# Decode attention on one core: K and V loaded in 1 MB transfers of 8 KB rows, four heads to a transfer and two transfers to a slot, slots on multiples of 512 bytes

## The chip, the cores and the metric

The kernel runs on one core of a Trainium2 chip. The metric is the device time of one execution in microseconds. Each run is called fast, or slow when it is over 1.5% above the fastest run of the same kernel.

In the profiles PE is the tensor engine (matrix products; PEld is its loading of weights), DVE the vector engine, ACT the scalar engine and SP the engine that issues the large loads. A load goes from HBM, the chip's main memory, to SBUF, the memory of 128 partitions beside the engines; 16 DMA engines carry it in packets. The granted PE clock is the share of full speed that the profile records for PE; "warm" means full clock, "cold" half.

## The reference

One decode step for 8 sequences: layer norm of `x`, attention over the last 1,024 cached tokens with 32 query heads on 8 key/value heads, and a gated feed-forward branch that multiplies the attention output.

```python
# x [8,1,512]; k_cache, v_cache [8, 8, 4096, 128]; all bf16
W = 1024                                   # min(4096, max(256, Sk // 4))
q = (layernorm(x) @ wq)                    # 32 heads of 128
k, v = k_cache[:, :, Sk-W:], v_cache[:, :, Sk-W:]   # each head serves 4 query heads
o = softmax(q @ k.T * 128**-0.5) @ v
s = o @ wo
g = silu((gelu(xn @ w_gate) * (xn @ w_up)) @ w_down)
return x + s * g
```

The tokens that are read of K and V are 33.6 MB; the weights are another 13.9 MB. Everything is read once.

## The kernel before

All large loads go through one DMA queue (the SP queue) into a ring of ten slots of 16 KB per partition. Weights are read with all 128 partitions as the outer dimension. A K or V tile is one batch, all 8 heads: partition `8p+n` holds 64 consecutive tokens of head `n`.

```python
PS = P // Hkv                     # 16 groups of 8 partitions
NCH = W // PS                     # 64 tokens in a partition
ring = tc.tile_pool(name="ring", bufs=10)
pad_t = pad.tile([P, 416 // 2], BF16)       # where the ring starts

def load_rows(src, rows, r0, n, name):      # weights
    t = ring.tile([P, n, src.shape[1]], BF16, tag="slot")
    nc.sync.dma_start(out=t, in_=src.rearrange("(p r) n -> p r n", r=rows)[:, r0:r0+n, :])

def load_cache(cache, b, name):             # K and V: 2 MB, rows of 16 KB
    t = ring.tile([P, NCH, Dh], BF16, tag="slot")
    nc.sync.dma_start(
        out=t.rearrange("p c d -> p (c d)"),
        in_=cache[b, :, win0:Sk, :].rearrange("n (p c) d -> p n (c d)", p=PS),
    )
# ... constants, layer norm, queries: cut ...
# per batch: 64 transposes of K (PE), 8 copies to SBUF (DVE), 4 mask matmuls,
# 64 score matmuls, 4 Exp (ACT), 4 sum matmuls, 64 value matmuls, 1 reduce, 1 scaling
for b in range(B):
    if b > 0:
        k_t[b] = load_cache(A_k_cache, b, "k_t")
        v_t[b - 1] = load_cache(A_v_cache, b - 1, "v_t")
    transposes(b, 0)
    # ... scores, values of the batch before, interleaved: cut ...
# ... feed-forward, output projection, final sum: cut ...
```

In memory the heads of a batch lie 1 MB apart, so the source of a K tile is 16 groups of 8 rows: rows of a group 1 MB apart, groups 16 KB apart.

The softmax here doesn't subtract the row's maximum and nothing guards it: scores larger than these inputs give would overflow.

Of the kernel before, what the change touches and what calls it, by code (L numbers as in the profile page):

```python
# [7 lines left out]
ACT = mybir.ActivationFunctionType  # L8
ALU = mybir.AluOpType
AX = mybir.AxisListType  # L10
BF16 = mybir.dt.bfloat16
FP32 = mybir.dt.float32

NEG = -1.0e30
# [3 lines left out]
def kernel(  # L18
# [13 lines left out]
    nc = tc.nc  # L32

    B, Sq, D = A_x.shape
    Hkv, Sk, Dh = A_k_cache.shape[1], A_k_cache.shape[2], A_k_cache.shape[3]
    Hq = A_wq.shape[1] // Dh
    rep = Hq // Hkv
    W = min(4096, max(256, Sk // 4))
    win0 = Sk - W
    F = B_w_gate.shape[1]  # L40
    P = nc.NUM_PARTITIONS
    KD = D // P
    FJ = F // P
    PS = P // Hkv
    NCH = W // PS
    GC = 16
    NGR = NCH // GC
    NQ = 4
    NW = D // NQ
    NT = 2  # L50
    HT = Hq // NT
    WI = HT * Dh // P
    WM = Dh // WI
    SLOT = NCH * Dh
    inv_sqrt_dh = float(Dh) ** -0.5

    x_flat = A_x.flatten_outer_dims()
# [2 lines left out]
    pad = ctx.enter_context(tc.tile_pool(name="pad", bufs=1))  # L60
    ring = ctx.enter_context(tc.tile_pool(name="ring", bufs=10))
    consts = ctx.enter_context(tc.tile_pool(name="consts", bufs=1))
    kT_pool = ctx.enter_context(tc.tile_pool(name="kT_pool", bufs=6))
    pT_pool = ctx.enter_context(tc.tile_pool(name="pT_pool", bufs=2))
    small = ctx.enter_context(tc.tile_pool(name="small", bufs=2))
    ps_k = ctx.enter_context(tc.tile_pool(name="ps_k", bufs=3, space=bass.MemoryType.PSUM))
    ps_s = ctx.enter_context(tc.tile_pool(name="ps_s", bufs=2, space=bass.MemoryType.PSUM))
    ps_o = ctx.enter_context(tc.tile_pool(name="ps_o", bufs=2, space=bass.MemoryType.PSUM))
    ps_t = ctx.enter_context(tc.tile_pool(name="ps_t", bufs=1, space=bass.MemoryType.PSUM))

    pad_t = pad.tile([P, 416 // 2], BF16, name="pad_t")

    def bank(pool, name, shape, dtype=FP32):
        return pool.tile(shape, dtype, name=name, tag=pool.name)
# [10 lines left out]
        out=xr[0:P:4, :], in_=x_flat.rearrange("b (q n) -> q b n", n=NW)  # L85
    )

    def load_rows(src, rows, r0, n, name):

        t = ring.tile([P, n, src.shape[1]], BF16, name=name, tag="slot")  # L90
        nc.sync.dma_start(out=t, in_=src.rearrange("(p r) n -> p r n", r=rows)[:, r0 : r0 + n, :])  # L91
        return t

    def load_cache(cache, b, name):
        t = ring.tile([P, NCH, Dh], BF16, name=name, tag="slot")
        nc.sync.dma_start(  # L96
            out=t.rearrange("p c d -> p (c d)"),
            in_=cache[b, :, win0:Sk, :].rearrange("n (p c) d -> p n (c d)", p=PS),
        )
        return t  # L100

    wq_t = [load_rows(A_wq, KD, k, 2, "wq_t") for k in (0, 2)]
    k_t, v_t = {}, {}
    k_t[0] = load_cache(A_k_cache, 0, "k_t")


    ident = consts.tile([P, P], BF16, name="ident")
    nc.vector.memset(ident, 0.0)
    nc.gpsimd.affine_select(
        out=ident, in_=ident, compare_op=ALU.not_equal, fill=1.0,  # L110
# [15 lines left out]
        out=xhat, in0=x_sb, scalar1=mv[:, 0:1], scalar2=rstd[:, 0:1],  # L126
        op0=ALU.subtract, op1=ALU.mult,
# [3 lines left out]
    for k in range(KD):  # L131
# [7 lines left out]
    ones_pp = consts.tile([P, P], BF16, name="ones_pp")  # L139
    nc.vector.memset(ones_pp, 1.0)  # L140

    sel8 = consts.tile([P, 8], FP32, name="sel8")
    nc.vector.tensor_reduce(
        out=sel8, in_=ident.rearrange("p (a n) -> p n a", n=8), axis=AX.X, op=ALU.add
# [3 lines left out]
        out=own16, in_=ident.rearrange("p (a n) -> p a n", n=8), axis=AX.X, op=ALU.add  # L148
    )
    selb = consts.tile([P, B], BF16, name="selb")  # L150
    nc.vector.tensor_copy(out=selb, in_=sel8)
    neg8 = consts.tile([P, Hkv], FP32, name="neg8")
    nc.vector.tensor_scalar(
        out=neg8, in0=sel8, scalar1=-1.0, scalar2=-NEG, op0=ALU.add, op1=ALU.mult
    )
    mask = consts.tile([P, GC, Hkv, rep], BF16, name="mask")
    nc.vector.tensor_copy(
        out=mask, in_=neg8.unsqueeze(1).unsqueeze(3).to_broadcast([P, GC, Hkv, rep])
    )
    ownm = consts.tile([P, HT, WM], BF16, name="ownm")  # L160
    nc.vector.tensor_copy(out=ownm, in_=own16.unsqueeze(2).to_broadcast([P, HT, WM]))
# [6 lines left out]
    qT = consts.tile([P, B, Hq], BF16, name="qT")  # L168
    qT_ps = bank(ps_s, "qT_ps", [P, Hq, B])
    for h in range(Hq):  # L170
        for k in range(KD):
# [4 lines left out]
                start=(k == 0),  # L176
                stop=(k == KD - 1),
# [2 lines left out]


    oT = consts.tile([P, NT, HT, B], BF16, name="oT")
    pT, kTs = {}, {}
    TG = 1024 // P

    def transposes(b, g):
        for t in range(GC // TG):
            kT_ps = bank(ps_k, "kT_ps", [P, TG * P], BF16)
            for i in range(TG):
                nc.tensor.transpose(  # L190
                    kT_ps[:, i * P : (i + 1) * P], k_t[b][:, g * GC + t * TG + i, :], ident
                )
            kT = kT_pool.tile([P, TG * P], BF16, name="kT")
            nc.vector.tensor_copy(out=kT, in_=kT_ps)  # L194
            kTs[b, g, t] = kT

    def scores(b, g):
        if g == 0:
            pT[b] = pT_pool.tile([P, NCH, Hq], BF16, name="pT")
        sc_ps = bank(ps_s, "sc_ps", [P, GC, Hq])  # L200
        nc.tensor.matmul(  # L201
            sc_ps.rearrange("p c h -> p (c h)"), ident, mask.rearrange("p c n j -> p (c n j)"),
            start=True, stop=False, skip_group_check=True,
        )
        for c in range(GC):
            nc.tensor.matmul(  # L206
                sc_ps[:, c, :], kTs[b, g, c // TG][:, (c % TG) * P : (c % TG + 1) * P], qT[:, b, :],
                start=False, stop=(c == GC - 1), skip_group_check=True,
            )
        nc.scalar.activation(  # L210
            out=pT[b][:, g * GC : (g + 1) * GC, :], in_=sc_ps, func=ACT.Exp, scale=inv_sqrt_dh
        )

    def values(b):
        oT_ps = bank(ps_o, "oT_ps", [P, Hq])
        sum_ps = bank(ps_t, "sum_ps", [P, GC, Hq])
        for g in range(NGR):
            nc.tensor.matmul(  # L218
                sum_ps.rearrange("p c h -> p (c h)"), ones_pp,
                pT[b][:, g * GC : (g + 1) * GC, :].rearrange("p c h -> p (c h)"),  # L220
                start=(g == 0), stop=(g == NGR - 1),
            )
        for c in range(NCH):
            nc.tensor.matmul(  # L224
                oT_ps, v_t[b][:, c, :], pT[b][:, c, :], start=(c == 0), stop=(c == NCH - 1)
            )
        sums = small.tile([P, Hq], FP32, name="sums")
        nc.vector.tensor_reduce(  # L228
            out=sums, in_=sum_ps.rearrange("p c h -> p h c"), axis=AX.X, op=ALU.add
        )  # L230
        nc.vector.reciprocal(out=sums, in_=sums)
        nc.vector.tensor_tensor(  # L232
            out=oT[:, :, :, b],
            in0=oT_ps.rearrange("p (t h) -> p t h", t=NT),
            in1=sums.rearrange("p (t h) -> p t h", t=NT),
            op=ALU.mult,
        )

    for b in range(B):
        if b > 0:  # L240
            k_t[b] = load_cache(A_k_cache, b, "k_t")
            v_t[b - 1] = load_cache(A_v_cache, b - 1, "v_t")
        transposes(b, 0)
        if b > 0:
            scores(b - 1, NGR - 1)
        transposes(b, 1)
        scores(b, 0)
        transposes(b, 2)
        scores(b, 1)
        if b > 0:  # L250
            values(b - 1)
        transposes(b, 3)
        scores(b, 2)

    wg_t = load_rows(B_w_gate, KD, 0, KD, "wg_t")
    wu_t = load_rows(B_w_up, KD, 0, KD, "wu_t")
    v_t[B - 1] = load_cache(A_v_cache, B - 1, "v_t")
    wd_t = load_rows(B_w_down, FJ, 0, FJ, "wd_t")
    wo_t = [[load_rows(A_wo[: HT * Dh, :], WI, 0, WI, "wo_t")]]
    LAST = 4  # L260
# [1 line left out]
        load_rows(A_wo[HT * Dh :, :], WI, 0, WI - LAST, "wo_t"),  # L262
        load_rows(A_wo[HT * Dh :, :], WI, WI - LAST, LAST, "wo_t"),
    ])
    scores(B - 1, NGR - 1)


    gu_ps = bank(ps_s, "gu_ps", [P, 2, FJ, B])
    for w, wt in enumerate((wg_t, wu_t)):
        for j in range(FJ):  # L270
            for k in range(KD):
# [4 lines left out]
                    start=(k == 0),  # L276
                    stop=(k == KD - 1),
# [6 lines left out]
        out=z2, in0=z2, scalar1=0.044715, scalar2=1.0, op0=ALU.mult, op1=ALU.add  # L284
# [6 lines left out]
        out=th, in0=th, scalar1=0.5, scalar2=0.5, op0=ALU.mult, op1=ALU.add  # L291
# [1 line left out]
    nc.vector.tensor_tensor(out=u3, in0=th, in1=zT, op=ALU.mult)  # L293
    nc.vector.tensor_tensor(out=hT[:, :, 0:32:4], in0=u3, in1=uT, op=ALU.mult)

    values(B - 1)



# [1 line left out]
    for t in range(NT):  # L301
# [6 lines left out]
            out=e,  # L308
            in0=o_sb.unsqueeze(2).to_broadcast([P, WI, HT, WM]),
            in1=ownm.unsqueeze(1).to_broadcast([P, WI, HT, WM]),  # L310
            op=ALU.mult,
# [5 lines left out]
    for j in range(FJ):  # L317
        for q in range(NQ):
            nc.tensor.matmul(  # L319
                f_ps[32 * q : 32 * (q + 1), :], hT[:, j, :], wd_t[:, j, q * NW : (q + 1) * NW],  # L320
                start=(j == 0), stop=(j == FJ - 1), tile_position=(0, 32 * q),
# [4 lines left out]
    for t in range(NT):  # L326
        r_ps = bank(ps_o, "r_ps", [P, WI, B])
        for i in range(WI):
            nc.tensor.matmul(  # L329
                r_ps[:, i, :], es[t][:, i, :, :].rearrange("p h m -> p (h m)"), selb,  # L330
                start=True, stop=True,
# [5 lines left out]
        out=th2, in0=th2, scalar1=0.5, scalar2=0.5, op0=ALU.mult, op1=ALU.add  # L337
# [5 lines left out]
    for t in range(NT):  # L343
        i = 0
        for w in wo_t[t]:
            for r in range(w.shape[1]):
                for q in range(NQ):
                    nc.tensor.matmul(  # L348
                        s_ps[32 * q : 32 * (q + 1), :], oR[:, t, i, :], w[:, r, q * NW : (q + 1) * NW],
                        start=(t == 0 and i == 0), stop=(t == NT - 1 and i == WI - 1),  # L350
# [9 lines left out]
        out=out_flat.rearrange("b (q n) -> q b n", n=NW), in_=out_sb[0:P:4, :]  # L360
# [31 lines left out]
```

## Time and profile before

| | before |
|---|---|
| time, median (range) of 3 runs | 200.45 us (199.37 to 203.18) |
| span of the profiled execution | 197.5 us |
| PE / DVE / ACT busy | 55% / 32% / 12% |
| DMA queue, share of 16 engines' span | 95.8% |
| GB/s while the query weights load / while K and V load | 423 / 209 to 252 |

The page of the kernel before: its span and engine line, then three lines of the span cut into 40 slices (granted PE clock and DMA busy share in tenths, GB/s moved), the main DMA queue (packets, MB, share of 16 engines), and the two cache loads (count, KB each, median us from issue to landing).

```profile
span 197.5 us, 4405 instructions
PE 107.9 (55%) x2053; PEld 93.7 (47%) x2062; DVE 63.2 (32%) x120; ACT 22.8 (12%) x38; POOL 1.4 (1%) x6
...
PEclk9999999696759685995798596859755896555555
DMA  6999999999999999999999999999999999999950
GB/s 224 423 358 212 209 212 212 209 216 209 216 216 216 212 211 216 229 242 219 245 229 252 216 229 226 226 219 226 229 222 219 231 413 295 219 234 410 423 240 6
...
q1 hardware_dynamic: 3492, 47.46, 95.8%
...
k_t<-in_A_k_cache_dram SPq DMA_DIRECT2D x8, 2048.0 KB, 70.5
v_t<-in_A_v_cache_dram SPq DMA_DIRECT2D x8, 2048.0 KB, 72.0
```

The DMA line reads 9 tenths or more nearly everywhere, so the engines are always busy. The GB/s line shows that busy is not fast: weights (slices 2, 33, 37, 38) move at over 400 GB/s, K and V at about half of that. A busy share cannot show this; the GB/s beside it can.

The waits view of before (engine, line, what it waited for: total us, times, longest):

```profile
PEld L190 <- DMA k_t<-in_A_k_cache_dram: 44.2, 8, 7.3
PE kT_ps L190 <- DMA k_t<-in_A_k_cache_dram: 43.4, 8, 7.2
...
PE oT_ps L224 <- DMA v_t<-in_A_v_cache_dram: 18.5, 8, 3.5
```

The tensor engine waits for K once in each of the 8 batches, for 43.4 us in total, and for V for 18.5 us.

### The profile page before, as it was taken

Reading aid. Unit: us, or ns where it says so; the run is one execution under the profiler, and the core shown is the slowest. Engines: PE = TensorE matmul, PEld = TensorE weight load, DVE = VectorE, ACT = ScalarE, POOL = GpSimd, SP = SyncE. Lnnn points to the kernel's source line nnn. Section 1 sums busy time; section 2 is a strip of 40 time slices with the busy share of each in tenths; the row PEclk is TensorE's granted clock in tenths of the full one; section 3 lists DMA queues with packets and bytes.
Section 4 is the critical chain, followed back from the end, with each engine's and each line's share of the span. In section 5 each row is a group of like instructions: output and inputs, shape, how many; then the busy total and the mean of one; then the engine's idle time right before and its main releaser. Section 6 shows DMA issues by size and latency. Waiting matters only on the chain.

```text
span 197.5 us, 4405 instructions
## 1 busy us (share of the span) xinstructions
PE 107.9 (55%) x2053; PEld 93.7 (47%) x2062; DVE 63.2 (32%) x120; ACT 22.8 (12%) x38; POOL 1.4 (1%) x6
## 2 busy tenths in 40 slices
PE   0015095938094809653971677177807777544552
PEld 0015094827083808543850557175707577524442
DVE  3300064543054305431641272137303730043501
ACT  5000012211012001210211020112001211010000
POOL 2000000000000000000000000000000000000000
PEclk9999999696759685995798596859755896555555
DMA  6999999999999999999999999999999999999950
GB/s 224 423 358 212 209 212 212 209 216 209 216 216 216 212 211 216 229 242 219 245 229 252 216 229 226 226 219 226 229 222 219 231 413 295 219 234 410 423 240 6
DMA packets 3561, 47.74 MB, mean 242 GB/s; under 512 B 464, under 2 KB 472, under 8 KB 600
## 3 DMA queue, kind: packets, MB, share of 16 engines
q1 hardware_dynamic: 3492, 47.46, 95.8%
q8 instruction: 16, 0.26, 0.6%
q10 hardware_dynamic: 52, 0.02, 0.0%
q14 instruction: 1, 0.01, 0.0%
HBM read 47.46 MB, written 0.01 MB: 240 GB/s over the span
## 4 chain that ended last, share of the span: by engine, by line
PE 45%; another core or an unknown queue 29%; DMA 21%; SPq 1%; issue 1%; DVE 0%
DMA v_t<-in_A_v_cache_dram 21%; PE kT_ps L190 18%; PE oT_ps L224 7%; PE sc_ps L206 5%; PE sc_ps L201 4%; PE gu_ps L272 4%; PE sum_ps L218 3%; PE s_ps L348 2%; PE f_ps L319 1%; SPq L96 1%; PE r_ps L329 0%; SPq L91 0%; PE o_ps L303 0%; DVE oT L232 0%
## 5 line engine op out<-in xcount | busy, mean ns | idle before, releaser
L190 PE MATMUL kT_ps<-ident,k_t 128*128 128x128 bf16 x512 | 48.7, 272 | 43.4 <-DMA k_t<-in_A_k_cache_dram 43.4
L194 DVE COPY kT<-kT_ps 128x1024 bf16<-128x1024 bf16 x64 | 42.9, 689 | 67.7 <-PE kT_ps L190 67.7
L190 PEld LDWEIGHTS <-k_t 128*128 128x128 bf16 x512 | 42.2, 125 | 44.2 <-DMA k_t<-in_A_k_cache_dram 44.2
L210 ACT ACTIVATE pT<-sc_ps 128x512 bf16<-128x512 f32 x32 | 19.1, 597 | 139.5 <-PE sc_ps L206 139.4
L224 PE MATMUL oT_ps<-pT,v_t 128*128 128x32 bf16 x512 | 14.4, 179 | 18.5 <-DMA v_t<-in_A_v_cache_dram 18.5
L224 PEld LDWEIGHTS <-v_t 128*128 128x128 bf16 x512 | 13.6, 98 | 22.9 <-DMA v_t<-in_A_v_cache_dram 22.9
L206 PEld LDWEIGHTS <-kT 128*128 128x128 bf16 x512 | 19.5, 102 | 6.4 <-issue 4.6
L206 PE MATMUL sc_ps<-qT,kT 128*128 128x32 bf16 x512 | 18.9, 182 | 0.2 <-issue 0.2
L201 PE MATMUL sc_ps<-mask,ident 128*128 128x512 bf16 x31 | 15.8, 510 | 0.0
L232 DVE TENSOR_TENSOR oT<-oT_ps,sums 128x32 bf16<-128x32 f32 x8 | 2.4, 301 | 24.0 <-PE oT_ps L224 24.0
L172 PE MATMUL qT_ps<-xnT,wq_t 128*128 128x8 bf16 x128 | 3.7, 168 | 8.9 <-DMA wq_t<-in_A_wq_dram 8.9
L172 PEld LDWEIGHTS <-wq_t 128*128 128x128 bf16 x128 | 3.6, 104 | 9.1 <-DMA wq_t<-in_A_wq_dram 9.1
L218 PE MATMUL sum_ps<-pT,ones_pp 128*128 128x512 bf16 x24 | 7.1, 410 | 0.7 <-issue 0.2
L228 DVE TENSOR_REDUCE sums<-sum_ps 128x32 f32<-128x512 f32 x8 | 5.5, 688 | 4.5 <-PE sum_ps L218 4.5
L348 PE MATMUL s_ps<-wo_t,oR 128*32 128x128 bf16 x128 | 3.8, 312 | 4.4 <-DMA wo_t<-in_A_wo_dram 4.4
L348 PEld LDWEIGHTS <-oR 128*32 128x32 bf16 x128 | 3.4, 143 | 4.6 <-issue 4.3
L272 PE MATMUL gu_ps<-xnT,wu_t 128*128 128x8 bf16 x56 | 3.5, 201 | 3.4 <-DMA wu_t<-in_B_w_up_dram 3.4
L272 PEld LDWEIGHTS <-wu_t 128*128 128x128 bf16 x56 | 3.4, 159 | 3.5 <-DMA wu_t<-in_B_w_up_dram 3.5
L201 PEld LDWEIGHTS <-ident 128*128 128x128 bf16 x32 | 4.1, 127 | 0.0
L179 DVE CAST qT<-qT_ps 128x256 bf16<-128x256 f32 x1 | 0.4, 425 | 11.0 <-PE qT_ps L172 11.0
L283 DVE TENSOR_SCALAR z<-z 128x112 f32<-128x112 f32 x1 | 0.2, 219 | 11.3 <-ACT z L282 11.3
L218 PEld LDWEIGHTS <-ones_pp 128*128 128x128 bf16 x32 | 2.7, 101 | 2.2 <-issue 0.5
(50 smaller groups left out, 31.2 us busy)
## 6 DMA issues: line engine op xcount, KB each, us to landing
k_t<-in_A_k_cache_dram SPq DMA_DIRECT2D x8, 2048.0 KB, 70.5
v_t<-in_A_v_cache_dram SPq DMA_DIRECT2D x8, 2048.0 KB, 72.0
wq_t<-in_A_wq_dram SPq DMA_DIRECT2D x2, 2048.0 KB, 10.1
wo_t<-in_A_wo_dram SPq DMA_DIRECT2D x1, 2048.0 KB, 58.4
wg_t<-in_B_w_gate_dram SPq DMA_DIRECT2D x1, 1792.0 KB, 70.9
wu_t<-in_B_w_up_dram SPq DMA_DIRECT2D x1, 1792.0 KB, 69.0
wd_t<-in_B_w_down_dram SPq DMA_DIRECT2D x1, 1792.0 KB, 63.1
wo_t<-in_A_wo_dram SPq DMA_DIRECT2D x1, 1536.0 KB
```

What stands on the lines that cost most here:

```text
L172: nc.tensor.matmul(qT_ps[:, h, :], wq_t[k // 2][:, k % 2, h * Dh : (h + 1) * Dh], xnT[:, k, :], start=(k == 0), stop=(k == KD - 1),)
L190: nc.tensor.transpose(kT_ps[:, i * P : (i + 1) * P], k_t[b][:, g * GC + t * TG + i, :], ident)
L194: nc.vector.tensor_copy(out=kT, in_=kT_ps)
L201: nc.tensor.matmul(sc_ps.rearrange("p c h -> p (c h)"), ident, mask.rearrange("p c n j -> p (c n j)"), start=True, stop=False, skip_group_ ...
L206: nc.tensor.matmul(sc_ps[:, c, :], kTs[b, g, c // TG][:, (c % TG) * P : (c % TG + 1) * P], qT[:, b, :], start=False, stop=(c == GC - 1), s ...
L210: nc.scalar.activation(out=pT[b][:, g * GC : (g + 1) * GC, :], in_=sc_ps, func=ACT.Exp, scale=inv_sqrt_dh)
L218: nc.tensor.matmul(sum_ps.rearrange("p c h -> p (c h)"), ones_pp, pT[b][:, g * GC : (g + 1) * GC, :].rearrange("p c h -> p (c h)"), start= ...
L224: nc.tensor.matmul(oT_ps, v_t[b][:, c, :], pT[b][:, c, :], start=(c == 0), stop=(c == NCH - 1))
L228: nc.vector.tensor_reduce(out=sums, in_=sum_ps.rearrange("p c h -> p h c"), axis=AX.X, op=ALU.add)
L232: nc.vector.tensor_tensor(out=oT[:, :, :, b], in0=oT_ps.rearrange("p (t h) -> p t h", t=NT), in1=sums.rearrange("p (t h) -> p t h", t=NT), ...
L272: nc.tensor.matmul(gu_ps[:, w, j, :], wt[:, k, :].rearrange("p (m j) -> p j m", j=FJ)[:, j, :], xnT[:, k, :], start=(k == 0), stop=(k == K ...
L348: nc.tensor.matmul(s_ps[32 * q : 32 * (q + 1), :], oR[:, t, i, :], w[:, r, q * NW : (q + 1) * NW], start=(t == 0 and i == 0), stop=(t == N ...
```

## The change

The stated intent: K and V in 1 MB transfers of 8 KB rows, 4 heads of a batch at a time; row `4p+n` holds 32 tokens of head `n`; two such halves share a slot; slots start on multiples of 512 bytes. The rest follows from it: a score tile now holds 4 heads' keys against 16 query heads, not 8 against 32, so there are half as many mask matmuls, Exp and sum matmuls, and twice as many (smaller) final reductions.

```diff
-    PS = P // Hkv
+    CS = 4
+    NH = Hkv // CS
+    HS = CS * rep
+    PS = P // CS
     NCH = W // PS
...
-    pad_t = pad.tile([P, 416 // 2], BF16, name="pad_t")
+    pad_t = pad.tile([P, 384 // 2], BF16, name="pad_t")
...
-    def load_cache(cache, b, name):
-        t = ring.tile([P, NCH, Dh], BF16, name=name, tag="slot")
+    def load_cache(cache, u, slots, name):
+        b, h = divmod(u, NH)
+        if h == 0:
+            slots[b] = ring.tile([P, NH, NCH, Dh], BF16, name=name, tag="slot")
         nc.sync.dma_start(
-            out=t.rearrange("p c d -> p (c d)"),
-            in_=cache[b, :, win0:Sk, :].rearrange("n (p c) d -> p n (c d)", p=PS),
+            out=slots[b][:, h, :, :].rearrange("p c d -> p (c d)"),
+            in_=cache[b, h * CS : (h + 1) * CS, win0:Sk, :].rearrange(
+                "n (p c) d -> p n (c d)", p=PS
+            ),
         )
...
-    mask = consts.tile([P, GC, Hkv, rep], BF16, name="mask")
+    mask = consts.tile([P, NCH, CS, rep], BF16, name="mask")
... (scores, values and the loop rewritten for 16 units of half a batch) ...
```

More of the change, by code (lines that the diff above doesn't have):

```diff
@@ L43 @@
     FJ = F // P
-    PS = P // Hkv
+    CS = 4
+    NH = Hkv // CS
+    HS = CS * rep
+    PS = P // CS
     NCH = W // PS
-    GC = 16
-    NGR = NCH // GC
+    TG = 8
+    NTG = NCH // TG
     NQ = 4
@@ L53 @@
     WM = Dh // WI
-    SLOT = NCH * Dh
     inv_sqrt_dh = float(Dh) ** -0.5
@@ L63 @@
     kT_pool = ctx.enter_context(tc.tile_pool(name="kT_pool", bufs=6))
-    pT_pool = ctx.enter_context(tc.tile_pool(name="pT_pool", bufs=2))
+    pT_pool = ctx.enter_context(tc.tile_pool(name="pT_pool", bufs=4))
     small = ctx.enter_context(tc.tile_pool(name="small", bufs=2))
@@ L92, in load_rows @@
         return t
-    def load_cache(cache, b, name):
-        t = ring.tile([P, NCH, Dh], BF16, name=name, tag="slot")
+    def load_cache(cache, u, slots, name):
+        b, h = divmod(u, NH)
+        if h == 0:
+            slots[b] = ring.tile([P, NH, NCH, Dh], BF16, name=name, tag="slot")
         nc.sync.dma_start(
-            out=t.rearrange("p c d -> p (c d)"),
-            in_=cache[b, :, win0:Sk, :].rearrange("n (p c) d -> p n (c d)", p=PS),
+            out=slots[b][:, h, :, :].rearrange("p c d -> p (c d)"),
+            in_=cache[b, h * CS : (h + 1) * CS, win0:Sk, :].rearrange(
+                "n (p c) d -> p n (c d)", p=PS
+            ),
         )
-        return t
     wq_t = [load_rows(A_wq, KD, k, 2, "wq_t") for k in (0, 2)]
     k_t, v_t = {}, {}
-    k_t[0] = load_cache(A_k_cache, 0, "k_t")
+    load_cache(A_k_cache, 0, k_t, "k_t")
     ident = consts.tile([P, P], BF16, name="ident")
@@ L140 @@
     nc.vector.memset(ones_pp, 1.0)
+    sel4 = consts.tile([P, CS], FP32, name="sel4")
+    nc.vector.tensor_reduce(
+        out=sel4, in_=ident.rearrange("p (a n) -> p n a", n=CS), axis=AX.X, op=ALU.add
+    )
     sel8 = consts.tile([P, 8], FP32, name="sel8")
@@ L151 @@
     nc.vector.tensor_copy(out=selb, in_=sel8)
-    neg8 = consts.tile([P, Hkv], FP32, name="neg8")
+    neg4 = consts.tile([P, CS], FP32, name="neg4")
     nc.vector.tensor_scalar(
-        out=neg8, in0=sel8, scalar1=-1.0, scalar2=-NEG, op0=ALU.add, op1=ALU.mult
+        out=neg4, in0=sel4, scalar1=-1.0, scalar2=-NEG, op0=ALU.add, op1=ALU.mult
     )
-    mask = consts.tile([P, GC, Hkv, rep], BF16, name="mask")
+    mask = consts.tile([P, NCH, CS, rep], BF16, name="mask")
     nc.vector.tensor_copy(
-        out=mask, in_=neg8.unsqueeze(1).unsqueeze(3).to_broadcast([P, GC, Hkv, rep])
+        out=mask, in_=neg4.unsqueeze(1).unsqueeze(3).to_broadcast([P, NCH, CS, rep])
     )
@@ L182 @@
     oT = consts.tile([P, NT, HT, B], BF16, name="oT")
-    pT, kTs = {}, {}
-    TG = 1024 // P
-    def transposes(b, g):
-        for t in range(GC // TG):
-            kT_ps = bank(ps_k, "kT_ps", [P, TG * P], BF16)
-            for i in range(TG):
-                nc.tensor.transpose(
-                    kT_ps[:, i * P : (i + 1) * P], k_t[b][:, g * GC + t * TG + i, :], ident
-                )
-            kT = kT_pool.tile([P, TG * P], BF16, name="kT")
-            nc.vector.tensor_copy(out=kT, in_=kT_ps)
-            kTs[b, g, t] = kT
@@ L197, in scores, with transposes @@
-    def scores(b, g):
-        if g == 0:
-            pT[b] = pT_pool.tile([P, NCH, Hq], BF16, name="pT")
-        sc_ps = bank(ps_s, "sc_ps", [P, GC, Hq])
+    pT, kTs, sc = {}, {}, {}
+    NU = B * NH
+    def transposes(u, t):
+        b, h = divmod(u, NH)
+        kT_ps = bank(ps_k, "kT_ps", [P, TG * P], BF16)
+        for i in range(TG):
+            nc.tensor.transpose(
+                kT_ps[:, i * P : (i + 1) * P], k_t[b][:, h, t * TG + i, :], ident
+            )
+        kT = kT_pool.tile([P, TG * P], BF16, name="kT")
+        nc.vector.tensor_copy(out=kT, in_=kT_ps)
+        kTs[u, t] = kT
@@ new lines, in scores @@
+    def scores(u, t):
+        b, h = divmod(u, NH)
+        if t == 0:
+            sc[u] = bank(ps_s, "sc_ps", [P, NCH, HS])
+            nc.tensor.matmul(
+                sc[u].rearrange("p c h -> p (c h)"), ident,
+                mask.rearrange("p c n j -> p (c n j)"),
+                start=True, stop=False, skip_group_check=True,
+            )
+        for i in range(TG):
+            nc.tensor.matmul(
+                sc[u][:, t * TG + i, :], kTs[u, t][:, i * P : (i + 1) * P],
+                qT[:, b, h * HS : (h + 1) * HS],
+                start=False, stop=(t == NTG - 1 and i == TG - 1), skip_group_check=True,
+            )
+        if t == NTG - 1:
+            pT[u] = pT_pool.tile([P, NCH, HS], BF16, name="pT")
+            nc.scalar.activation(out=pT[u], in_=sc[u], func=ACT.Exp, scale=inv_sqrt_dh)
@@ L201, in scores, with values @@
+    def values(u):
+        b, h = divmod(u, NH)
+        oT_ps = bank(ps_o, "oT_ps", [P, HS])
+        sum_ps = bank(ps_t, "sum_ps", [P, NCH, HS])
         nc.tensor.matmul(
-            sc_ps.rearrange("p c h -> p (c h)"), ident, mask.rearrange("p c n j -> p (c n j)"),
-            start=True, stop=False, skip_group_check=True,
-        )
-        for c in range(GC):
-            nc.tensor.matmul(
-                sc_ps[:, c, :], kTs[b, g, c // TG][:, (c % TG) * P : (c % TG + 1) * P], qT[:, b, :],
-                start=False, stop=(c == GC - 1), skip_group_check=True,
-            )
@@ L210, in scores @@
-        nc.scalar.activation(
-            out=pT[b][:, g * GC : (g + 1) * GC, :], in_=sc_ps, func=ACT.Exp, scale=inv_sqrt_dh
-        )
-    def values(b):
-        oT_ps = bank(ps_o, "oT_ps", [P, Hq])
-        sum_ps = bank(ps_t, "sum_ps", [P, GC, Hq])
-        for g in range(NGR):
-            nc.tensor.matmul(
-                sum_ps.rearrange("p c h -> p (c h)"), ones_pp,
-                pT[b][:, g * GC : (g + 1) * GC, :].rearrange("p c h -> p (c h)"),
-                start=(g == 0), stop=(g == NGR - 1),
-            )
+            sum_ps.rearrange("p c h -> p (c h)"), ones_pp, pT[u].rearrange("p c h -> p (c h)"),
@@ L223, in values @@
+            start=True, stop=True,
+        )
         for c in range(NCH):
             nc.tensor.matmul(
-                oT_ps, v_t[b][:, c, :], pT[b][:, c, :], start=(c == 0), stop=(c == NCH - 1)
+                oT_ps, v_t[b][:, h, c, :], pT[u][:, c, :], start=(c == 0), stop=(c == NCH - 1)
             )
-        sums = small.tile([P, Hq], FP32, name="sums")
+        sums = small.tile([P, HS], FP32, name="sums")
         nc.vector.tensor_reduce(
@@ L231, in values @@
         nc.vector.reciprocal(out=sums, in_=sums)
-        nc.vector.tensor_tensor(
-            out=oT[:, :, :, b],
-            in0=oT_ps.rearrange("p (t h) -> p t h", t=NT),
-            in1=sums.rearrange("p (t h) -> p t h", t=NT),
-            op=ALU.mult,
-        )
-    for b in range(B):
-        if b > 0:
-            k_t[b] = load_cache(A_k_cache, b, "k_t")
-            v_t[b - 1] = load_cache(A_v_cache, b - 1, "v_t")
-        transposes(b, 0)
-        if b > 0:
-            scores(b - 1, NGR - 1)
-        transposes(b, 1)
-        scores(b, 0)
-        transposes(b, 2)
-        scores(b, 1)
-        if b > 0:
-            values(b - 1)
-        transposes(b, 3)
-        scores(b, 2)
+        nc.vector.tensor_tensor(out=oT[:, h, :, b], in0=oT_ps, in1=sums, op=ALU.mult)
+    for u in range(NU):
+        if u > 0:
+            load_cache(A_k_cache, u, k_t, "k_t")
+            load_cache(A_v_cache, u - 1, v_t, "v_t")
+        transposes(u, 0)
+        if u > 0:
+            scores(u - 1, NTG - 2)
+        transposes(u, 1)
+        if u > 0:
+            scores(u - 1, NTG - 1)
+        transposes(u, 2)
+        scores(u, 0)
+        if u > 1:
+            values(u - 2)
+        transposes(u, 3)
+        scores(u, 1)
     wg_t = load_rows(B_w_gate, KD, 0, KD, "wg_t")
     wu_t = load_rows(B_w_up, KD, 0, KD, "wu_t")
-    v_t[B - 1] = load_cache(A_v_cache, B - 1, "v_t")
+    load_cache(A_v_cache, NU - 1, v_t, "v_t")
     wd_t = load_rows(B_w_down, FJ, 0, FJ, "wd_t")
@@ L264 @@
     ])
-    scores(B - 1, NGR - 1)
+    scores(NU - 1, NTG - 2)
+    scores(NU - 1, NTG - 1)
+    values(NU - 2)
     gu_ps = bank(ps_s, "gu_ps", [P, 2, FJ, B])
@@ L294 @@
     nc.vector.tensor_tensor(out=hT[:, :, 0:32:4], in0=u3, in1=uT, op=ALU.mult)
-    values(B - 1)
+    values(NU - 1)
     es = []
```

## The prediction

> **What bounds the kernel now.** The DMA queue. The page's DMA line is at 9 tenths in slices 2 to 38; the queue table gives the SP queue 95.8% of sixteen engines' span. But these busy engines move two rates: the GB/s line shows 410 to 423 for most of the weights and 209 to 252 for K and V. In the packet records a 16 KB packet of the query weights takes 611 ns, one of K or V mostly 1,080 to 1,295 ns. K and V are 33.6 of 47.5 MB and about 155 of the 197.5 us. No compute engine is near its limit: PE 55%, DVE 32%, ACT 12%; in the waits view the transposes wait 43.4 us for K, the value products 18.5 us for V.
>
> **Why half rate (my reading).** Every large load has 128 partitions. The source's slowest dimension is 16 in K and V (8 rows, one per head, inside), 128 in the weights. [...]
>
> **What the change does.** Row 4p+n makes that dimension 32 with 4 rows each[...]. [...] From 159 ns for 4 KB and 611 for 16 KB I estimate 310 ns for 8 KB, 423 GB/s: halving the packets costs nothing. Slot alignment: under 2%; weights already make 429 GB/s.
>
> Compute gets lighter: mask and sum matmuls 4 to 2 per batch (0.21 us each at full clock), Exp 4 to 2 (597 ns); the sums reduce goes 1 to 2 (688 ns), with one more reciprocal (353) and scaling (301). Transposes (16 in 0.90 us warm, 1.89 cold), score and value matmuls keep their count. Estimate per batch: PE 7.8 us warm, 12.2 at half clock, DVE 8, against 9.9 us for 4.19 MB at 423 GB/s. PE comes close, but ten slots let DMA run some 40 us ahead.
>
> **Sum.** 47.46 MB at 400 to 423 GB/s is 112 to 119 us; start 1.5; tail after the last landing 5.5 (192.0 to 197.5 now); 3 from span to reported time: 122 to 129. I predict **126 us**. If [...]the half rate has another cause (the 1 MB pitch between heads stays), the time stays 196 to 201; I give that a quarter. Range **119 to 201**; faster 0.72, same 0.24, slower 0.04.
>
> **What would show it.** Right: GB/s about 400 throughout, 8 KB packets about 310 ns, waits for K shrinking, PE busy 75% or more and mostly at full clock. Wrong: GB/s still 210 to 250, 8 KB packets 600 to 650 ns. Between (135 to 160): GB/s near 420 in bursts, the DMA queue waiting for slots that half-clock transposes hold.
>
> **What would make it wrong.** [...] PE kept cold; gaps between transfers.

112 to 119 us for the bytes, 1.5 for the start, 5.5 for the tail and 3 from span to reported time make 122 to 129 us, and 126 is near the middle.

## More of the kernel before

The windows view of before in three stretches of 5 us (busy us and instruction count of each engine, granted clock, DMA share, GB/s): query weights, the middle, and the output weights.

```profile
5.00:10.00 5.00, 0.22 (x2) 0.13 (x2) 1.43 (x8) 0.10 (x1) 0.00 (x0) 1.00 1.03 437
40.00:45.00 5.00, 1.96 (x49) 1.30 (x48) 1.75 (x4) 0.60 (x1) 0.00 (x0) 1.00 0.99 210
180.00:185.00 5.00, 3.08 (x98) 2.61 (x95) 3.24 (x5) 0.19 (x1) 0.00 (x0) 0.50 1.00 426
```

The DMA share is about 1.00 in all three, the rate 437, 210 and 426 GB/s.

## The result, and the profile after

The kernel after took 122.90 us (median of 4 runs, 122.85 to 122.97). Before, the runs beside it included, has a median of 201.43 us (199.37 to 203.18). The ratio is 0.6148, with a 95% interval of 0.6119 to 0.6177. Ratios here are the mean time of one kernel's fast runs over that of the other's of the same rounds, so not quite the ratio of the medians quoted.

| | before | after |
|---|---|---|
| span of the profiled execution | 197.5 us | 121.1 us |
| DMA queue share | 95.8% | 93.3% |
| HBM read over the span | 240 GB/s | 392 GB/s |
| PE / DVE busy share | 55% / 32% | 70% / 58% |
| mean granted PE clock | 0.762 | 0.874 |
| PE waits for K (transposes) | 43.4 us | 12.7 us |

The page of the kernel after, the same lines:

```profile
span 121.1 us, 4374 instructions
PE 85.1 (70%) x2030; PEld 78.2 (65%) x2030; DVE 69.7 (58%) x145; ACT 13.3 (11%) x22; POOL 1.4 (1%) x6
...
PEclk9999999999999999999999996579999955555555
DMA  4999999999999999999999999999999999999710
GB/s 100 428 435 431 411 427 419 430 422 427 419 425 425 425 425 419 427 422 425 419 430 417 433 417 430 427 419 425 422 436 438 417 417 445 428 428 415 290 68 3
...
q1 hardware_dynamic: 5796, 47.46, 93.3%
...
k_t<-in_A_k_cache_dram SPq DMA_DIRECT2D x16, 1024.0 KB, 20.0
v_t<-in_A_v_cache_dram SPq DMA_DIRECT2D x16, 1024.0 KB, 20.3
```

The DMA line has hardly changed. The GB/s line is flat at 411 to 445 from slice 2 to slice 37: K and V now move at the weights' rate. The bytes are the same 47.46 MB.

The waits view of after:

```profile
PEld L200 <- DMA k_t<-in_A_k_cache_dram: 13.8, 12, 2.2
PE kT_ps L200 <- DMA k_t<-in_A_k_cache_dram: 12.7, 12, 2.1
```

The longest wait for K fell from 7.2 to 2.1 us, and the view lists no wait of the value matmuls for V any more.

The windows view of after, in the query weights, the middle, and a stretch in which the PE clock fell while K and V were loading (it falls again near the end):

```profile
5.00:10.00 5.00, 0.21 (x2) 0.13 (x2) 1.50 (x8) 0.00 (x0) 0.00 (x0) 1.00 1.02 434
40.00:45.00 5.00, 4.12 (x106) 3.80 (x104) 3.78 (x8) 0.60 (x1) 0.00 (x0) 1.00 1.02 431
75.00:80.00 5.00, 5.00 (x85) 4.45 (x84) 3.19 (x6) 0.60 (x1) 0.00 (x0) 0.50 1.01 424
```

In the middle PE is busy 4.12 of 5 us and DVE 3.78, both below the DMA. Between 75 and 80 us PE is full at half clock, and the DMA goes on at 424 GB/s: the loads in flight carry it over.

The chain of work that ended last, by engine, from the page of after:

```profile
DMA 84%; PE 12%; DVE 0%; SPq 0%; issue 0%
```

The kernel is still bound by the DMA queue, at twice the rate for K and V.

The packet records of the two traces say the same in the smallest unit (duration of one packet, percentiles over the stretch where K and V load; my own count from the trace's packet records):

```
kernel   stretch us   packet    p10    median   p90   ns      GB/s of these
before   25 to 150    16 KB    1054      1213  1289                221
after    15 to 85      8 KB     309       309   309                422
both     6 to 10      16 KB     611       611   611-612  (query weights)
```

### The profile page after: what moved, and what is told of

Its sections match the earlier page's. It is cut to its first block, busy times and chain, and to the rows that moved or that the text cites. A ratio compares the mean times of both kernels' runs of the same rounds, so it can differ in the third digit from the quotient of the medians.

```text
span 121.1 us, 4374 instructions
## 1 busy us (share of the span) xinstructions
PE 85.1 (70%) x2030; PEld 78.2 (65%) x2030; DVE 69.7 (58%) x145; ACT 13.3 (11%) x22; POOL 1.4 (1%) x6
## 3 DMA queue, kind: packets, MB, share of 16 engines
q1 hardware_dynamic: 5796, 47.46, 93.3%
HBM read 47.46 MB, written 0.01 MB: 392 GB/s over the span
## 4 chain that ended last, share of the span: by engine, by line
DMA 84%; PE 12%; DVE 0%; SPq 0%; issue 0%
DMA k_t<-in_A_k_cache_dram 51%; DMA wo_t<-in_A_wo_dram 24%; DMA wq_t<-in_A_wq_dram 10%; PE kT_ps L200 6%; PE sc_ps L217 2%; PE s_ps L357 2%; PE oT_ps L235 1%; PE sc_ps L211 1%; PE sum_ps L230 1%; SPq L93 0%; DVE tmp L365 0%; DVE out_sb L367 0%; SPq L101 0%
## 5 line engine op out<-in xcount | busy, mean ns | idle before, releaser
L200 PE MATMUL kT_ps<-ident,k_t 128*128 128x128 bf16 x512 | 41.5, 229 | 12.7 <-DMA k_t<-in_A_k_cache_dram 12.7
L200 PEld LDWEIGHTS <-k_t 128*128 128x128 bf16 x512 | 31.4, 102 | 14.0 <-DMA k_t<-in_A_k_cache_dram 13.8
L217 PE MATMUL sc_ps<-qT,kT 128*128 128x16 bf16 x512 | 22.3, 170 | 0.4 <-DVE kT L204 0.4
L224 ACT ACTIVATE pT<-sc_ps 128x512 bf16<-128x512 f32 x16 | 9.6, 597 | 80.7 <-PE sc_ps L217 80.7
L235 PE MATMUL oT_ps<-pT,v_t 128*128 128x16 bf16 x512 | 15.6, 170 | 0.0
L239 DVE TENSOR_REDUCE sums<-sum_ps 128x16 f32<-128x512 f32 x16 | 11.0, 690 | 1.1 <-PE sum_ps L230 1.1
L211 PE MATMUL sc_ps<-mask,ident 128*128 128x512 bf16 x16 | 6.3, 396 | 0.0
L243 DVE TENSOR_TENSOR oT<-oT_ps,sums 128x16 bf16<-128x16 f32 x16 | 3.7, 229 | 2.1 <-PE kT_ps L200 0.5
L242 DVE RECIPROCAL sums<-sums 128x16 f32<-128x16 f32 x16 | 4.0, 253 | 0.5
L281 PE MATMUL gu_ps<-xnT,wg_t 128*128 128x8 bf16 x56 | 3.5, 201 | 0.7 <-DMA wg_t<-in_B_w_gate_dram 0.7
```

The source lines that it names most:

```text
L200: nc.tensor.transpose(kT_ps[:, i * P : (i + 1) * P], k_t[b][:, h, t * TG + i, :], ident)
L211: nc.tensor.matmul(sc[u].rearrange("p c h -> p (c h)"), ident, mask.rearrange("p c n j -> p (c n j)"), start=True, stop=False, skip_group_ ...
L217: nc.tensor.matmul(sc[u][:, t * TG + i, :], kTs[u, t][:, i * P : (i + 1) * P], qT[:, b, h * HS : (h + 1) * HS], start=False, stop=(t == NT ...
L224: nc.scalar.activation(out=pT[u], in_=sc[u], func=ACT.Exp, scale=inv_sqrt_dh)
L235: nc.tensor.matmul(oT_ps, v_t[b][:, h, c, :], pT[u][:, c, :], start=(c == 0), stop=(c == NCH - 1))
L239: nc.vector.tensor_reduce(out=sums, in_=sum_ps.rearrange("p c h -> p h c"), axis=AX.X, op=ALU.add)
```

## The experiments

Theory 1 has two steps. First, the grouping of the source's rows decides the rate: K and V in 16 groups of 8 rows run at half rate, in 32 groups of 4 rows they run as the weights do. Second, the half rate depends on how the DMA engines run against each other in time. Theory 2 says that packet size, transfer size or alignment is what helps. Theory 3 says that it is the HBM side: the 1 MB pitch between heads. Eleven kernels were run, and the kernel after once more. No trace says which engine carried a packet.

Three kernels read wrong tokens (said with each). They were still counted correct, most likely because attention enters the result as a small correction to `x`, too small for the comparison to see. For these runs only the time is used.

### b_rows_4p: the grouping alone

```diff
-            in_=cache[b, :, win0:Sk, :].rearrange("n (p c) d -> p n (c d)", p=PS),
+            in_=cache[b, 0:4, Sk - 2 * W : Sk, :].rearrange("n (p c) d -> p n (c d)", p=32),
```

This is the kernel before; every instruction on every engine is the same but for the source of these loads (wrong tokens).

> The kernel before with one thing changed: K and V are fetched as 4 heads x 2048 tokens, row 4p+n, so the source's slowest dimension is 32 instead of 16. Transfers stay 2 MB, packets 16 KB, slots where they were, all compute the same (wrong result on purpose). Theory 1 (row grouping decides[...]): K/V packets fall from about 1,280 to about 611 ns, GB/s about 420 throughout, time 122 to 130 us. Theory 2 (packet size, transfer size or slot alignment decides): stays at 197 to 203 us. Theory 3 (the 1 MB pitch between heads costs the rate): stays slow, since the pitch stays.

Measured: 123.36 us (123.35 to 123.42), ratio to before 0.6148 (0.6119 to 0.6178). The GB/s line of its page:

```profile
GB/s 105 421 433 432 431 431 420 431 426 420 431 426 426 420 431 412 431 420 426 415 431 410 431 420 431 420 420 431 420 422 412 439 416 420 420 424 411 268 66 3
```

K and V packets of 16 KB took 612 to 621 ns (p10 to p90). The first step of theory 1 holds, theories 2 and 3 fail for the main effect: with 2 MB transfers, 16 KB rows, the old slot offset, all of the old compute and the 1 MB pitch kept, the ratio is that of the whole change.

### b_two_halves: 1 MB transfers of 8 KB rows, old grouping

```diff
+        src = cache[b, :, win0:Sk, :].rearrange("n (p c) d -> p n (c d)", p=PS)
...
+        for i in (0, 1):
+            nc.sync.dma_start(out=dst[:, i * half : (i + 1) * half],
+                              in_=src[:, :, i * half : (i + 1) * half])
```

> The kernel before with each 2 MB K or V load cut into two 1 MB loads of 8 KB rows; the grouping stays 16 groups of 8 rows (right result). Theory 1: 8 KB packets take 600 to 650 ns, GB/s 210 to 250, time 196 to 203 us. Theory 2 (1 MB transfers of 8 KB rows are what helps): packets about 310 ns, time below 135 us.

Measured: 189.13 us (185.10, 188.45, 189.81, 191.46), against 198.41 to 203.81 for before in the same rounds. The GB/s line of its page (the run of 185.1 us):

```profile
GB/s 220 413 377 225 220 222 222 223 227 220 223 220 227 232 234 265 274 257 288 259 281 274 257 257 252 254 247 268 256 250 244 343 386 217 247 313 425 417 177 5
```

Theory 2 fails: packets had a median of 622 ns between 15 and 60 us, where 309 would be full rate. But my range of 196 to 203 was missed too: from slice 16 to slice 31 the rate is 244 to 288. b_four_quarters takes this up.

### b_no_pitch: the 1 MB pitch taken away

```diff
+        rows = cache[b].rearrange("n s d -> (n s) d")[0 : PS * 521, :]
+        src = rows.rearrange("(p r) d -> p r d", r=521)[:, 0:520, :]
+        src = src.rearrange("p (n c) d -> p n c d", c=65)[:, :, 0:NCH, :]
...
```

The kernel before with the rows of a group 16.25 KB apart (wrong tokens).

> The kernel before with the 1 MB pitch between heads taken away: the 8 rows of a group lie 16.25 KB apart in memory, groups 130 KB apart, still 16 groups of 8 rows of 16 KB (wrong result on purpose). Theory 1: no change, 16 KB packets mostly 1,050 to 1,300 ns, 196 to 203 us. Theory 3 (HBM and its pitch): packets near 611 ns, below 135 us.

Measured: 201.25 us (200.41 to 203.65), ratio to before 1.0015 (0.9940 to 1.0090).

```profile
GB/s 226 430 346 211 214 211 221 217 231 221 211 217 211 213 234 217 217 217 217 211 211 221 224 224 224 211 234 217 231 214 211 237 404 305 208 215 394 415 301 7
```

Theory 3 in the form "the pitch costs the rate" fails. Without the pitch the rate stays at 211 to 234 GB/s from slice 4 to slice 31; with it b_rows_4p loads at 410 to 439 from slice 2 to slice 37.

### b_phase and b_phase_control: the same K and V loads, engines set out of step

```diff
+    for groups in (4, 12):
+        t = ring.tile([P, NCH, Dh], BF16, name="shift", tag="slot")
+        nc.sync.dma_start(
+            out=t[0 : 4 * groups].rearrange("p c d -> p (c d)"),
+            in_=A_k_cache[0, 0:4, 0 : groups * NCH, :].rearrange("n (p c) d -> p n (c d)", p=groups),
+        )
```

The two loads were meant to occupy 4 and 12 engines, and so to put the engines out of step; the landings listed under b_phase_8_engines show that they did. The control loads the same bytes in two loads of 16 groups, as K and V have them: in the kernel before, each K tile has 16 landings.

> The kernel before, K and V loads untouched, but two loads of data nobody reads go ahead of them, 256 KB on 4 groups and 768 KB on 12 groups[...] (right result). Theory 1[...]: [...] K/V packets fall to 611 to 800 ns for most of the run, time 125 to 155 us although 1 MB more is loaded. If only [...]the source pattern matters[...]: 199 to 206 us.

> The control of b_phase: the same 256 KB and 768 KB of unread data ahead of K and V, but spread over 16 groups like the K tiles[...] (right result). Theory 1[...]: no relief, packets 1,050 to 1,300 ns, 200 to 208 us. If b_phase gained from something else (extra transfers, slots shifted by two): a time near b_phase's 167 to 185 us.

Measured: b_phase 175.66 us (167.24, 172.21, 179.11, 184.76), although it loads 1 MB more; b_phase_control 207.10 us (204.44 to 207.92), ratio to before 1.0274 (1.0154 to 1.0394). Even the slowest b_phase is below the fastest before (198.41). The GB/s lines, b_phase first (its profiled run is the slowest, 184.76 us):

```profile
GB/s 220 413 401 204 197 387 383 387 383 312 301 283 261 274 279 276 261 265 301 301 279 326 322 279 283 225 190 211 195 287 202 257 209 256 207 377 328 109 27 5
```

```profile
GB/s 242 428 311 247 208 211 208 224 218 215 211 221 221 211 216 221 221 221 205 227 221 218 224 218 234 231 237 224 221 231 215 246 407 252 211 225 346 425 258 10
```

In slices 6 to 9 of b_phase, 23 to 40 us, the untouched K and V loads run at 383 to 387 GB/s, with a median of 632 ns for a 16 KB packet. No K or V load was changed. Between b_phase and its control only the shape of the two small loads differs, and in b_phase the engines finish the first K tile in three bunches, at 22.93 to 23.27, 25.29 to 25.80 and 28.22 to 28.48 us. So the shape of the K and V loads alone does not fix the half rate; that it is how the engines run against each other in time is my reading. My range of 125 to 155 us was missed: the relief was nearly full but lasted some 17 us, then the rate fell to 261 to 326 (slices 10 to 25) and later to 190 to 287 (slices 26 to 35). What ended the relief is not shown.

### b_phase_8_engines: only four engines set back

```diff
-    for groups in (4, 12):
+    for groups in (4,):
```

> b_phase with only the first of its two loads (256 KB on 4 groups[...])[...]. [...] K/V packets fall in two classes early on, about half of them at 611 to 700 ns and the others at 1,200 to 1,300; each transfer still ends with its slow half, so GB/s stays near 215 and the time at 194 to 204 us, with the mean DMA busy share below 9 tenths in that stretch. [...]

Measured: 198.09 us (196.69 to 201.69), ratio to before 0.9932 (0.9814 to 1.0051).

```profile
GB/s 220 435 359 218 215 215 215 218 225 225 238 235 242 242 277 228 235 232 222 232 225 228 228 225 235 232 222 232 235 225 217 262 412 206 230 207 402 419 262 6
```

The time was met, the two classes of packets were not: between 15 and 46 us the 16 KB packets took 1,085 to 1,265 ns (p10 to p90), one class, all slow, and the DMA share did not fall. Not one of these packets took less than 1,026 ns. Only between about 50 and 75 us did a part of them fall below 800 ns. The set-back did happen, as the trace's semaphore updates show: I read them as one by the issuer, then one for each engine that finishes its share (us from the span's start). The first K tile of the kernel before has 16 landings, at 22.79 to 24.56 us.

```
b_phase_8_engines
  4-group load    2.81 (issuer)   then 17.85 17.92 18.22 18.49
  first K tile    22.32 22.33 22.43 22.48 22.52 22.60 22.60 22.62 22.64 22.69 22.92
                  24.54   then 27.37 27.53 27.67 28.24
b_phase
  12-group load   3.73 (issuer)   then 17.59 17.72 17.84 17.86 17.95 18.04 18.05 18.30
                                  then 22.96 23.04 23.04 23.14
  first K tile    22.93 23.05 23.19 23.27   then 25.29 25.39 25.41 25.47 25.48 25.52 25.80
                                  then 28.22 28.25 28.32 28.35 28.48
```

By these landings four engines carried the small load and twelve the other. In b_phase_8_engines the last four engines finish the K tile 5 us after the first eleven, about four slow packets later, and yet no packet got faster. The lag lasted: two tiles on, the last four landings come at 46.30 to 47.15 us, the first ten at 41.29 to 41.73.

The reading called for two classes of packets here, and named one class as the outcome that would speak against it: one class came. In b_phase, where the landings of the first K tile come in bunches of 4, 7 and 5, K and V ran at 383 to 387 GB/s for a time. Here, with four engines late and twelve nearly together, every packet stayed slow. So the second step of theory 1 does not hold as I put it: that four engines are out of step is not enough to free even a part of the packets. Why b_phase relieved the queue and this run did not is not shown.

### a_rows_8p: only the grouping undone in after

```diff
-            in_=cache[b, h * CS : (h + 1) * CS, win0:Sk, :].rearrange(
-                "n (p c) d -> p n (c d)", p=PS
+            in_=cache[b, :, win0 + h * W // 2 : win0 + (h + 1) * W // 2, :].rearrange(
+                "n (p c) d -> p n (c d)", p=16
```

(wrong result: the tokens land in the wrong rows for the mask)

> The kernel after with only the grouping undone: each 1 MB load takes 8 heads x 512 tokens in 8 KB rows, row 8p+n, 16 groups of 8; transfers, packets, slots, alignment and compute as in after (wrong result on purpose). Theory 1: as b_two_halves, 8 KB packets mostly 350 to 650 ns, GB/s 220 to 290, 180 to 195 us. Theory 2 (8 KB rows, 1 MB, alignment, lighter compute): stays at 123 to 130 us.

Measured: 182.44 us (180.66 to 185.42), ratio to before 0.9097 (0.9009 to 0.9184).

```profile
GB/s 219 422 382 228 232 230 232 241 235 232 244 235 241 234 234 244 250 281 270 284 272 261 277 261 255 259 264 252 252 252 254 253 366 359 230 327 438 415 133 5
```

As theory 1 expects. With b_rows_4p this shows the grouping from both sides: alone it brings the gain, and without it the rest of the change leaves 182 us.

### a_half_parts and a_half_cols: half the partitions, or half the columns, at a time

```diff
...
+        for i in (0, 1):     # a_half_parts
+            nc.sync.dma_start(out=dst[64 * i : 64 * (i + 1)], in_=src[16 * i : 16 * (i + 1)])
```
```diff
...
+        for i in (0, 1):     # a_half_cols
+            nc.sync.dma_start(out=dst[:, 2048 * i : 2048 * (i + 1)],
+                              in_=src[:, :, 2048 * i : 2048 * (i + 1)])
```

Both are the kernel after with 512 KB transfers; every byte goes where it went, and both results are right.

> The kernel after, each K or V load cut into two loads of 512 KB, one to partitions 0 to 63 and one to 64 to 127; every byte goes to the same place as in after (right result). The source keeps its groups of 4 rows. Theory 1[...]: [...] 8 KB packets of 350 to 650 ns and 180 to 200 us, although no row moved. If the source's reading pattern sets the rate: 122 to 130 us.

> The control of a_half_parts: the kernel after, each K or V load cut into two loads of 512 KB by columns, all 128 partitions in each, 4 KB rows (right result). Theory 1: packets about 159 ns, 123 to 128 us. If 512 KB transfers or twice the number of them cost the rate in a_half_parts: as slow as that one, or at least above 140 us.

Measured: a_half_parts 191.20 us (189.68 to 192.34), ratio to before 0.9539 (0.9458 to 0.9620); a_half_cols 124.24 us (124.16 to 124.35), ratio 0.6215 (0.6183 to 0.6247). The GB/s lines, a_half_parts first:

```profile
GB/s 222 442 341 224 224 229 224 222 222 225 225 232 225 229 232 222 229 225 227 222 230 225 230 234 232 232 229 229 232 234 232 234 318 428 303 341 419 415 180 5
```

```profile
GB/s 94 423 436 427 403 422 414 419 415 419 415 419 411 422 412 418 416 414 419 418 415 420 418 416 420 408 424 415 418 437 447 413 413 436 434 422 428 306 76 3
```

With the rows of after, written 64 partitions at a time, the rate is halved (222 to 234 GB/s from slice 4 to slice 32); with the same transfer size over all 128 partitions it is kept (403 to 447 from slice 2 to slice 37), packets of 4 KB at 159 ns, and the time is 1.3 us above the 122.9 of after. So 512 KB transfers are not what halves it. Whether the 64 partitions do or the 16 groups of 4 rows that such a load has is not shown: the run changed both. Against the distance of the groups in memory speaks b_no_pitch: it moved the groups from 16 to 130 KB apart as well, and the rate stayed at 211 to 234.

### b_four_quarters: why b_two_halves was not at 200

The edit is that of b_two_halves with four transfers of 512 KB and 4 KB rows.

> The kernel before with each K or V load cut into four loads of 512 KB with 4 KB rows, still 16 groups of 8 rows (right result). It asks why b_two_halves ended at 185 to 191 us and not at 200. Theory: [...] 160 to 182 us, below b_two_halves, with GB/s at 250 to 290 from early on. If b_two_halves gained from a fixed effect of the cut: 185 to 195 us. If short packets alone bring the full rate: below 135 us.

Measured: 176.08 us (164.82, 175.89, 176.28, 185.32), against 198.35 to 203.73 for before in the same rounds. The GB/s line of its profiled run (175.89 us):

```profile
GB/s 194 434 399 239 237 236 234 237 235 242 244 247 248 250 260 270 282 272 283 271 273 270 262 264 271 271 275 272 281 287 281 368 393 244 289 329 423 411 184 6
```

The time lies in the range and the rate goes from about 236 to 262 to 287; but it takes 65 us to get there, not "early on". The argument that led to the range rested on the second step, against which b_phase_8_engines speaks. So the closeness may be luck. The fastest runs of the three cuts are 198.35, 185.10 and 164.82 us for one (the kernel before), two and four transfers: the more cuts, the faster. The cause is not shown, nor is what lets the rate rise in the course of a run.

### after_again and a_pad416: the alignment

```diff
-    pad_t = pad.tile([P, 384 // 2], BF16, name="pad_t")
+    pad_t = pad.tile([P, 416 // 2], BF16, name="pad_t")
```

> The kernel after, unchanged, as the yardstick for a_pad416 on the same chip: 122.5 to 123.3 us.

> The kernel after with its slots back at the offset of before (pad of 416 bytes instead of 384), all else the same. Alignment costs little: in b_rows_4p, in the old slots, 16 KB packets took 612 to 621 ns where aligned ones would take twice 309, so 8 KB packets should take 309 to 318 ns; 122.8 to 124.5 us, slower than after by 0 to 1.2%. If the 512-byte slots carry part of the gain: over 126 us.

Measured: after 122.91 us (122.87 to 123.09), ratio to before 0.6180 (0.6161 to 0.6199); a_pad416 124.72 us (124.64 to 125.05), ratio 0.6270 (0.6251 to 0.6290). Six runs each. The GB/s line of a_pad416's page:

```profile
GB/s 120 395 439 424 427 427 413 424 413 419 408 421 416 416 424 411 413 413 424 411 419 416 421 408 421 419 416 419 416 425 424 434 411 421 439 417 409 272 73 3
```

The aligned slots are worth 1.8 us, or 1.5%: 8 KB packets take 311 to 320 ns (p10 to p90) in the old slots and 309 in the new ones. That is a little more than I allowed, and with the new grouping in place it is the only other part of the change whose gain was measured by itself.

One 2 MB transfer per batch in the new row order, with the right tokens, was not run.

## Why the prediction was right

- **The DMA queue at half rate as the bound: right.** The gain came from the rate alone: 47.46 MB at 240 GB/s over the span before, 392 after.
- **The cause, first step (16 groups of 8 rows against 32 groups of 4): right.** That the grouping decides the rate is shown by b_rows_4p (123.36 us) and a_rows_8p (182.44), with the pitch and the sizes ruled out as the main cause by b_no_pitch (201.25) and b_two_halves (185.10 at best). How the grouping acts is not shown: the landings show how many engines a load used (4 and 12 in b_phase), not which rows each got.
- **The cause, second step (how the engines run against each other): in part.** That the same K and V loads can run at 383 to 387 GB/s or at half, by what goes ahead of them, is shown by b_phase and its control. That the engines out of step run fast and the others slow is contradicted by b_phase_8_engines: one class of packets, 1,085 to 1,265 ns. The time needed only the first step: any cause that goes with the grouping would have given 126 us, so 122.9 is no evidence for the second.
- **8 KB packets, estimate 310 ns: right.** Measured 309.
- **Alignment, under 2%: right.** 1.5%.
- **Compute, PE 7.8 us and DVE 8 us per batch: right.** In the window from 40 to 45 us PE is busy 4.12 and DVE 3.78 of 5 us; a batch of 4.19 MB takes 9.9 us at 424 GB/s, which makes 8.2 and 7.5 us. PE was busy 70% of the span, not the 75% that I named: it does little in the first 12 us.
- **"Ten slots let DMA run some 40 us ahead": wrong, without effect.** The DMA queue's own waits view in after:

```profile
SPq L101 <- DMA k_t<-in_A_k_cache_dram: 24.9, 13, 2.1
SPq L101 <- DMA v_t<-in_A_v_cache_dram: 23.2, 11, 3.1
```

  It waits for landings of earlier loads, and the issues are 2.45 us apart with 20.0 us to land: eight transfers in flight, about 20 us ahead, although ten slots hold twenty of 1 MB. With the same ten slots b_rows_4p, in 2 MB transfers, issues every 4.9 us with 37.5 us to land, and a_half_cols, in 512 KB, issues two every 2.5 us with 10.1 us to land: eight again. So my 40 us fits 2 MB transfers, and the change halved it. Twenty us were enough for the half-clock stretch from 75 to 80 us.
- **The sum, 126 us against 122.9.** Two terms were too large. I took 3 us from span to reported time, out of two different executions (200.45 and 197.5); in one and the same execution it is 1.8 (122.92 and 121.1). I allowed 116 us for the bytes, 409 GB/s; from 1.5 us to the last landing that PE waits for, at 115.6, they took 114.1, 416 GB/s. The tail was right: 5.5 us from there to the end at 121.1. The range of 119 to 201 also held the old time, so that the result lies in it says little; the 126 and the reasons are what was tested.

What the other parts are worth together can be read from b_rows_4p: the old compute, old slots and 16 KB rows with the new grouping take 123.4 us, 0.5 more than the whole change. The whole change but for the alignment (a_pad416) takes 124.7: in the old slots, 8 KB rows, 1 MB transfers and lighter compute together gain nothing (they cost 1.3 us), and the alignment then brings 1.8 us back. That the lighter compute shows no gain fits the profile, in which no compute engine is the limit; it was not tested by itself.

## What to carry to other kernels

Put GB/s beside the DMA busy share, and compare it with another load of the same kernel: engines can be 95.8% busy with most of the bytes at half rate, and no wait points at the cause. Then look at the source's outer dimension: here 32 groups of 4 rows and 128 single rows ran at full rate (422 and 429 GB/s by their packets) and 16 groups of 8 at half (221; no other grouping of 128 rows was tried), and loads over 64 of the 128 partitions ran at half rate too (222 to 234). With the new grouping and a full queue, packet size and transfer size mattered little, down to 4 KB rows and 512 KB transfers (1.3 us of 122.9). With the old grouping smaller transfers helped in part: 198.4, 185.1 and 164.8 us in the fastest runs with 2 MB, 1 MB and 512 KB.
